# Another order table for a fused linear-attention and gated-MLP kernel on one core

## The chip, the cores and the metric

The kernel runs on one core of a Trainium2 chip. The metric is the device time of one execution in microseconds (us). A core has five engines that take their instructions in order, each from a queue of its own: TensorE (PE, matmuls; its weight loads are listed as PEld), VectorE (DVE), ScalarE (ACT), GpSimd (POOL) and SyncE (SP, which here issues nearly all DMAs). Semaphores order them against each other. Matmul results stand in eight PSUM banks; all other tiles stand in SBUF.

## The reference

There are two parts. The first is a recurrence for 4 batches and 8 heads over 768 positions with head size 48; the second is a gated MLP over all heads joined (width 384).

```
# attention, per batch b and head h
state = alpha[t][:, None] * state + outer(k[t], v[t])      # 48 x 48
y[t]  = q[t] @ state
# MLP, x = y of all heads joined: (4, 768, 384)
h = relu(x @ w_in)                       # 384 -> 1024
u, v = h[..., :512], h[..., 512:]
v_n = (v - mean(v)) / sqrt(var(v) + 1e-6)
v_s = einsum('ts,bsd->btd', w_spatial, v_n) + b_spatial    # mixes positions, 768 x 768
out = (u * v_s) @ w_out                  # 512 -> 384
```

All inputs and the output are float32.

## The kernel before

The sequence is cut into 24 chunks of 128 positions, six for each of the four batches. Inside a chunk the recurrence is written as matmuls: alpha's logarithms are summed by a triangular matmul (`cum`), their exponentials scale q and k (`qt`, `kt`), the scaled q and k are transposed (`tr`, `trk`), multiplied with each other (`sc`), masked (`m`, `ms`) and multiplied with v (`y`); the state that a chunk adds is a matmul of k and v (`upd`), which DVE and POOL carry on (`z`, `S`, `sb`). Chunks 0 to 3 and 6 to 9 are done four at a time with positions interleaved, chunks 4 and 5 as a pair, and all others singly. A batch's chunk outputs (`xe`) then go through the MLP: `v` and `u` products with their ReLU copies (`ve`, `ue`), statistics (`bn`, `rs`, `nm`, `vn`), mixing over positions (`s`, with `se` and the gate product `g`) and the output product (`o`, copied by `oe`, stored by `st`). Weights arrive as float32, are cast to bf16, and the spatial weight is also transposed (`wt`, copied by `we`).

Matmuls use TensorE in several shapes: the full 128x128 array (most MLP products), 64x128 (transposes and `sc`), 128x32 (`y`), 32x32 (`pm`, which rearranges v), 32x128 (`upd` of four chunks), 64x32 and 64x64 (the pair).

The kernel first makes a list of 944 operations. Each has its dependencies, the engines that may run it and a function that emits its instructions. The order of all instructions then comes from one string, `PLAN`. The function `replay` goes through its words from left to right:

```
        op, eng = ops[int(word[1:])], LETTERS[word[0]]
        for x in junk:
            warm(int(cols), int(n), kind)
        for slot, n in zip(op.take, banks):
            held[n] = slot
        op.emit(eng)
```

So `A116` emits operation 116 on ACT, `P410@1,6` emits 410 on PE into banks 1 and 6, and `P62@0:512#0` first emits a dummy float32 matmul of 512 columns into bank 0. The letters D, G and S stand for DVE, POOL and SP. The words of one engine give its queue; the order between engines is left to semaphores. A PE operation that takes a bank waits for the copies that emptied the bank's last content.

The words that the text below speaks of:

| word | operation |
|---|---|
| P62, P66, P75 | running sums of the first four chunks' logarithms |
| P52 | spreads b_spatial over partitions |
| P115, A116 / P128, A129, A135 | v of chunk 0 rearranged and copied / the same of chunks 2 and 3 |
| A102 | copy of transposed q (chunks 0 to 3) |
| A173, A176, A178, A180 | logarithm and exponentials of the pair, chunks 4 and 5 |
| P120, P419 | output of chunk 0, of chunk 10 |
| S12, S16 | loads of w_in, v half and u half |
| S20, S23, S26, S29 | loads of w_spatial in thirds, and of w_out |
| P154, P156, P160 | u products of batch 0, first half of the positions |
| P217, P221 | u products of batch 0, second half |
| S278 | last load of chunks 6 to 9 (v) |
| S494, S560, A564 | alpha loads of chunks 12 and 15, logarithm of chunk 15 |
| P293, A294, G306 | running sum, exponential and scaled key in chunks 6 to 9 |
| G299, G302 | copies of v in chunks 6 to 9 |
| P321, D322 (S.6) | state update of chunks 6 to 9, and its first scaling |
| P410 | transposes of chunks 10 and 11 |

The float32 loads of the weights share two staging buffers, so that a load waits for the casts of the load two before it; the loads of alpha, k, q and v go to a ring of three places.

Of the kernel before, what the change touches and what calls it, by code (L numbers as in the profile page):

```python
# [39 lines left out]


PLAN = """
D2 D0 D4 D1 G9 G11 G5 G6 D3 S56 S57 S59 S58 A60 S12 S169 S170 A61 S275 S171 D8 P62@0:512#0:512#0:512#0 P66@1 P67 P63
P70@2 P71 P74@3 P75 A68 A64 D79 G82 P91@4,5 P52@6 A69 A72 A76 G7 A78 A92 A84 A65 G88 G87 A73 A77 D85 D90 D81 D93 D53
D83 D80 P103@6,4,5,7:512#7:424#7 P94@0,1 D86 D104 D89 D106 G13 P97@6,2:192#2 D98 A95 P100@3,0 D101 A96 P117@3,6:376#1
P115@4,1 A99 G107 G14 A15 A173 D102 D109 P128@0,2 D119 D118 P174@5 A116 A122 A176 P130@6,4 S16 D132 D131 S172 A135
P175@1 A129 P120@3 P54@2 G110 G105 P136@0,4 A121 A178 A55 G111 G108 P133@6 G181 A180 A134 G184 A179 D112 A177 D138
P123@7,3 P141@2 S20 G279 G280 G281 G17 G19 G18 D124 D125 P151@6 P187@7,4 P126@3 S23 S277 S276 D185 A152 A127 G186 G183
G113 G114 D182 P190@5,6 A189 A192 A142 P144@3 D137 P139@4 D188 D191 A140 G22 G21 D153 D143 P199@6,5 P196@2,7 P162@4
A283 A145 P290@0 A163 P154@1 P160@3 A282 A291 A155 D200 D201 D198 D197 D164 P193@4 A161 P156@7 A157 A165 D194 D146  # L50
P158@5 A159 G195 P202@1,2 P203 S26 A204 A147 D166 P293@4 P37@5,7 D38 P34@3,6 G24 S278 S387 S399 G25 S506 S29 D35
P207@1 D148 D208 D36 A39 A292 P205 P284@7 P40@3,5 A206 A285 A167 G10 D42 P210@2 D149 D150 D41 S388 S389 D168 D209 S401
S400 P287@5 P223@6 P219@3 P221@1 A211 A294 A224 A288 D212 A286 A220 A213 D298 D304 A289 A295 D214 D222 D215 A216
P225@6 P233@2 P217@3 P229@7 P237@0 A218 A28 D301 G300 G27 D307 G297 P226 D227 G303 G306 P43@3,5 D45 P230 P234 D231
D235 A296 A44 P46@4,6 P309@5,1 D311 P238 P49@7,3 D50 D51 A48 A47 A310 P312@2,6 P318@1,4 P315@5,7 P249@3 P250 A313 A319
A317 A299 A314 A302 D316 D320 D239 G236 D251 P341@4,1 P335@7,5 P245@0 P246 G305 G308 D336 D342 G232 P321@7,6,3,2 G240
G228 D343 D322 A510 G33 D337 D324 D247 P253@4 P333@7,1 P254 P241@5 P242 G323 A391 A403 A30 A340 A334 A32 G325 P392@0
D255 P348@7,6 D243 D327 D350 A393 P344@4 A394 P338@5 G31 G328 D397 D330 D349 G396 P404@3 A345 A339 A405 A406 P257@1
A395 S495 S390 A258 P260@4 P359@2 S402 G407 G248 G326 G329 S494 S560 P346@0,7 D408 P354@3,5 P410@1,6 A360 D331 A347
A353 A411 D356 D355 P362@2 G252 G398 P351@7 A352 P357@3 D412 S508 S497 S509 P421@6,1 P416@5,0 D361 S496 S507 S562 S550  # L60
S548 S611 S561 S551 S549 A358 A363 D418 D423 P511@7 P369@3 P413@0 P374@2 P380@1 D414 D417 A261 A512 P378@0 D422 A498
D364 A375 A564 P263@5 P499@6 G244 G332 G409 G256 A370 A379 A513 D371 G415 A500 A501 P419@0 P424@3 A425 G517 G505 G503
D381 D382 D516 G515 A420 P266@2 P269@4 A502 A365 A383 A270 D366 D504 P429@0 P426@1 P438@3 P440@6 D384 A368 A430 A427
P436@4 A437 A441 A385 D264 D439 P272@0 D367 D267 D428 D431 D386 P521@1 P372@4 A514 A273 P565@6 P376@2 A377 A432 A552
P442@7 A568 P529@0 D443 D522 P456@3 D433 D434 A435 A566 A567 D373 P452@7 P553@1 P518@2,5 A519 A554 A556 D520 A555 P457
D458 D530 D570 G569 G523 G557 G459 P444@4 P445 P448@5 D446 P453 D454 P468@6 P449 D558 D450 P533@7,4 P524@2,0 P572@1,3
D525 G451 G455 P472@5 P469 P460@2 P473 D526 D534 D535 G531 G447 D474 S623 A559 P575@7 D576 A573 P461 S625 S612 S563
A615 D470 D462 P616@4 P527@5 P536@1 A627 S613 A574 P579@7,3 P588@6,0 G577 A617 A528 D589 A618 A537 P628@5 A629 A571
G475 P538@2 A630 P464@1 S624 S614 S730 S718 S721 S626 S720 G620 D621 D581 D580 S733 S732 P476@6 G631 G578 P541@3
P584@7 A539 A619 A542 P465 S784 S719 A477 D632 P634@5,4 D590 A636 D466 D585 S731 A722 P591@3 S786 S772 S785 S773 S835  # L70
S774 A592 S787 S775 G622 G532 P582@1 A583 D635 D540 P637@7 P482@6 A633 A483 P723@5 G586 G471 D638 G639 A724 P645@3,4
P640@0,2 D543 G463 G587 P479@7 P604@6 P596@1 D646 D642 D641 A734 A726 D647 G729 G467 A605 A741 G727 P593@3 P600@6 A594
P735@0 D606 D595 A738 D480 P648@4 P643@3 A544 D545 D546 D597 A649 P488@2 A644 A788 A601 A489 D547 P653@4 P660@7 P745@6
A654 D746 D655 A736 A607 D608 D610 P491@3 P664@4 A661 A665 A737 P650@6 A492 A776 G739 P598@1 D651 D609 P485@4 D652
A486 A725 D747 P666@7 A667 D740 P602@6 P662@4 P789@3 A656 A603 P676@7 P672@0 P753@6 A599 A790 A791 P777@1 A778 A792
A779 S484 S847 S836 S837 A839 A783 S838 S848 A663 S849 D657 D658 D659 D754 D728 P677 P673 P680@6 P688@5 D674 P681
P668@0 D794 D755 D678 D782 G781 G795 D682 P799@7 P669 G793 D800 P689 G675 D690 D670 P742@6,4 P796@7,3 A851 A780 D797
P696@5 A743 A798 G683 G679 P808@0 P697 P852@7 P840@6 A841 A842 A853 A843 A854 D744 P748@3,4 P757@1,2 D698 G801 G671
D749 D809 D758 P692@5 P693 D694 D750 P684@3 P703@0 P685 P700@5 G846 D759 A701 D686 P706@4 D856 D845 D707 A704 P760@5
A761 P751@0 A752 A802 P803@6,7 D805 G844 G855 P812@3,2 P858@4,5 G810 G687 G699 G691 A859 G695 D813 P762@0 S850 P861@7  # L80
P765@3 D814 D804 P712@2 P815@6 A756 A763 P806@0 A860 D862 D764 D857 A816 A807 A766 P864@5,7 P869@4,1 S702 P715@6 D866
D871 D767 D870 D865 P828@7 A829 D830 P824@1 P820@3 P817@7 A821 A768 A818 A825 G863 P872@4 A873 S705 A716 S481 S259
S268 S487 S265 S493 S490 S271 S708 S262 S478 S274 G811 P867@5 D819 P826@3 P822@1 D868 P877@4 D769 D771 A827 S717 A831
A823 A878 A770 A713 D832 P874@3 D833 D834 P890@5 P888@1 P884@4 D879 D875 D876 A880 D881 D882 P916@6 P709@2 A710 P896@3
P886@7 P900@0 A887 A889 A885 A891 P892@2 D883 P897 D898 G899 P893 P901 P908@5 P909 D894 D902 P904@2 P905 G903 P917
P912@0 P913 P920@3 D906 D895 D918 G919 D907 P929@6 P923@2 P921 S711 A930 S931 A924 S925 S714 D914 D910 D911 P926@6
G915 D922 P932@2 A933 D927 S928 S934 P938@3 D939 S940 P935@6 A936 S937 P941@3 D942 S943
"""


# [1174 lines left out]
```

## Time and profile before

| | |
|---|---|
| runs | 138.22, 138.32, 139.34 us; median 138.32 |
| span of the profiled execution | 137.9 us (no other time is given for it) |
| instructions in the profile | 5298 |
| first matmul that isn't a dummy | 6.37 us after the span's start |
| DMA | 28.66 MB in 76521 packets, mean 208 GB/s |
| loads of one chunk of alpha, k, q or v | 192.0 KB, median 4.2 to 4.4 us from issue to landing |
| granted TensorE clock | 9 tenths or more in every slice |

The times in the profile count from the span's start. A row of the timeline gives start, length, engine, line, operation, output and inputs with their shapes, and how many instructions of one kind were merged in it; in brackets stands the idle time before it and what ended it. Starts are measured; the ends of matmuls are modelled, so that the distance between starts is what a matmul costs in a stream. A row of busy time by stage gives the stretch, its length, each engine's busy time with the number of its instructions, the granted clock, the DMA share and the DMA rate.

### The profile page before, as it was taken

What the parts mean: (1) busy time and instruction counts of PE and PEld (TensorE: products, weight loads), DVE (VectorE), ACT (ScalarE), POOL (GpSimd) and SP (SyncE); (2) the same over time, 40 slices, a digit from 0 to 9 for tenths busy, and PEclk for the clock granted to TensorE, in tenths of its full rate; (3) what the DMA queues carried; (4) which work ended last, traced back from release to release, by engine and by line L of the source; (5) the groups of instructions that cost most, each with busy time, mean ns of one, the idle gap of its engine ahead of it and who ended that gap; (6) DMA issues with size and microseconds to landing.
All of it is one profiled execution on the core that took longest, in us unless ns stands there. A gap on an engine that the chain in (4) does not pass through costs nothing.

```text
span 137.9 us, 5298 instructions
## 1 busy us (share of the span) xinstructions
PE 130.1 (94%) x2108; PEld 79.4 (58%) x2122; DVE 120.2 (87%) x300; ACT 107.7 (78%) x261; POOL 86.6 (63%) x146
## 2 busy tenths in 40 slices
PE   6999998999999999799999999999999999999990
PEld 3365555565566556466657676656576765566560
DVE  6259999989989999899899999997999999974960
ACT  3476998999999799699997989999865796953040
POOL 7355899993499799761079989520799841004550
PEclk9999999999999999999999999999999999999999
DMA  3999999499989788699999898999960597101064
GB/s 88 370 372 381 344 349 361 106 373 382 355 162 281 159 168 165 124 186 188 193 204 201 164 209 156 189 186 216 213 134 5 187 349 270 63 0 57 0 233 172
DMA packets 76521, 28.66 MB, mean 208 GB/s; under 512 B 63056, under 2 KB 74960, under 8 KB 76496
## 3 DMA queue, kind: packets, MB, share of 16 engines
q1 hardware_dynamic: 76464, 28.32, 77.8%
q8 instruction: 16, 0.26, 0.8%
q14 instruction: 9, 0.07, 0.2%
q0 software_dynamic: 32, 0.00, 0.0%
HBM read 23.60 MB, written 4.72 MB: 205 GB/s over the span
## 4 chain that ended last, share of the span: by engine, by line
PE 60%; DMA 19%; POOL 8%; issue 3%; SPq 3%; ACT 3%; DVE 0%; POOLq 0%; ACTq 0%
PE bank L1005 43%; DMA raw_w<-in_moe_w_spatial_dram 6%; DMA kc<-in_k_dram 5%; DMA raw_w<-in_moe_w_out_dram 4%; DMA ac<-in_alpha_dram 4%; PE bank L960 3%; SPq L883 3%; PE bank L944 2%; PE bank L988 2%; PE bank L416 2%; POOL w_row L180 2%; POOL kt L189 2%; PE bank L932 1%; PE bank L898 1%; POOL state L189 1%
## 5 line engine op out<-in xcount | busy, mean ns | idle before, releaser
L1005 PE MATMUL bank<-w_spT,vn 128*128 128x384 bf16 x192 | 35.6, 327 | 0.0
L189 POOL TENSOR_TENSOR gT<-vs,uT 128x384 bf16<-128x384 f32 x28 | 25.7, 933 | 14.1 <-DVE vs L1152 14.1
L189 POOL TENSOR_TENSOR kt<-kc,binv 128x384 bf16<-128x384 f32 x22 | 20.2, 928 | 22.3 <-ACT binv L908 15.2
L1005 PEld LDWEIGHTS <-vn 128*128 128x128 bf16 x192 | 17.5, 98 | 11.2 <-issue 0.3
L1005 PE MATMUL bank<-w_in,xT 128*128 128x512 bf16 x58 | 17.4, 380 | 1.6 <-ACT xT L178 0.7
L1005 PE MATMUL bank<-xT,w_in 128*128 128x384 bf16 x96 | 18.7, 326 | 0.0
L1005 PE MATMUL bank<-w_out_sb,gT 128*128 128x384 bf16 (+1 forms) x100 | 18.4, 320 | 0.0
L1152 DVE TENSOR_TENSOR vs<-bank,bsp_bc 128x384 f32<-128x384 f32 x31 | 16.3, 549 | 2.4 <-PE bank L1005 2.3
L949 DVE TENSOR_TENSOR ptm<-bank,mask 128x512 bf16<-128x512 f32 x28 | 17.9, 682 | 0.5 <-PE bank L944 0.3
L178 ACT COPY kqT<-bank 128x512 bf16<-128x512 bf16 (+1 forms) x20 | 15.0, 793 | 3.1 <-PE bank L988 1.9
L1067 DVE BATCH_NORM_STATS2 stats<-v_sb 128x6 f32<-128x512 bf16 x24 | 16.4, 683 | 0.6 <-ACT v_sb L184 0.5
L184 ACT ACTIVATE v_sb<-bank 128x512 bf16<-128x512 f32 x20 | 11.7, 597 | 2.0 <-PE bank L1005 1.7
L184 ACT ACTIVATE uT<-bank 128x384 bf16<-128x384 f32 x27 | 12.4, 494 | 0.7 <-PE bank L1005 0.6
L1005 PEld LDWEIGHTS <-w_in 128*128 128x128 bf16 x96 | 9.0, 97 | 6.7 <-DVE ptm L949 0.3
L189 DVE TENSOR_TENSOR qt<-qc,bank 128x384 bf16<-128x384 f32 x24 | 12.6, 545 | 0.2 <-DMA qc<-in_q_dram 0.2
L1005 PEld LDWEIGHTS <-gT 128*128 128x128 bf16 x100 | 9.2, 98 | 5.8
L178 ACT CAST xT<-bank 128x384 bf16<-128x384 f32 x23 | 10.4, 482 | 1.1 <-PE bank L416 0.8
L843 DVE TENSOR_TENSOR ptm<-bank,mask 128x512 bf16<-128x512 f32 x16 | 10.3, 683 | 0.2 <-PE bank L836 0.2
L242 PE MATMUL bank<-junk 128*128 128x512 f32 (+3 forms) x14 | 8.8, 763 | 1.0 <-DVE junk L1231 1.0
L1005 PEld LDWEIGHTS <-xT 128*128 128x128 bf16 x72 | 6.2, 97 | 6.2 <-ACT xT L178 1.2
L178 ACT COPY raw_w<-bank 128x384 f32<-128x384 f32 x8 | 3.8, 479 | 7.3 <-PE bank L1005 7.2
L393 DVE TENSOR_TENSOR zs<-bank,state 128x384 f32<-128x384 f32 x16 | 8.8, 548 | 0.5 <-PE bank L932 0.4
(162 smaller groups left out, 264.3 us busy)
## 6 DMA issues: line engine op xcount, KB each, us to landing
ac<-in_alpha_dram SPq DMA_DIRECT2D x14, 192.0 KB, 4.4
kc<-in_k_dram SPq DMA_DIRECT2D x14, 192.0 KB, 4.4
qc<-in_q_dram SPq DMA_DIRECT2D x14, 192.0 KB, 4.4
vc<-in_v_dram SPq DMA_DIRECT2D x14, 192.0 KB, 4.2
raw_w<-in_moe_w_spatial_dram SPq DMA_DIRECT2D x3, 768.0 KB, 7.8
out_dram<-raw_w SPq DMA_DIRECT2D x11, 192.0 KB, 2.1
out_dram<-o_sb SPq DMA_DIRECT2D x9, 192.0 KB, 2.0
ac<-in_alpha_dram SPq DMA_DIRECT2D x2, 768.0 KB, 6.7
```

The costliest lines, as they stand in the source:

```text
L178: nc.scalar.copy(out=out, in_=in_)
L184: nc.scalar.activation(out=out, in_=in_, func=AF.Relu)
L189: ENG[eng].tensor_tensor(out=out, in0=in0, in1=in1, op=ALU.mult)
L242: nc.tensor.matmul(out=banks[n][:, 0:cols].rearrange("p (a b) -> p a b", a=4), lhsT=junk, rhs=junk[:, None, 0:cols // 4].to_broadcast([128 ...
L393: lambda _: nc.vector.tensor_tensor(out=zs[i % 3], in0=tp(), in1=state[(i - 1) % 3], op=ALU.add),
L843: nc.vector.tensor_tensor(out=ptm[n2][:, ci, s], in0=banks[sl.bank].rearrange("p (hp t) -> p hp t", hp=HP), in1=mask[:, 3][:, None, :].to_ ...
L883: nc.sync.dma_start(out=t[x].rearrange("p hp s d -> p (hp s) d"), in_=src[b, :, c * C:c * C + C, :].rearrange("h s d -> s h d"))
L949: nc.vector.tensor_tensor(out=ptm[n2][:, ci, s], in0=banks[sl_p[s].bank].rearrange("p (hp t) -> p hp t", hp=HP), in1=mask[:, 2][:, None, : ...
L960: nc.tensor.matmul(out=place(to, 3 * hp + (0, 1, 1, 2)[x]), lhsT=heads(vb, hp, x), rhs=ptm[n2][:, ci, x // 2, hp, :], start=(turn == 0), s ...
L1005: nc.tensor.matmul(out=ps, lhsT=lhsT, rhs=rhs, start=first and n == 0, stop=last and n == len(pairs) - 1)
L1067: nc.vector.bn_stats(out=stats[tt % 2], in_=v_sb[n2][:, tt, :])
L1152: nc.vector.tensor_tensor(out=vs[d], in0=banks[sl.bank][:, 0:TH], in1=bsp_bc[:, th, :], op=ALU.add)
```

## The change

Only `PLAN` is new. Its 944 words name the same operations. No operation, tile or dependency is added or removed. What differs:

- the order on all five engines, and with it the bank numbers;
- the engine of some elementwise operations: DVE has 225 words in place of 235, ACT 240 in place of 234, POOL 115 in place of 111; PE has 265 and SP 99 as before;
- the dummy matmuls: before they were 512, 512, 512 | 512, 424 | 192 | 376 columns, and they are 512, 512, 512, 120 | 328 | 512 | 144 | 456 | 288 | 248 | 512, 96 (a bar parts places in the order);
- successive PE words of different tile shape: 78 places in place of 85, dummies counted as the full shape.

```diff
 PLAN = """
-D2 D0 D4 D1 G9 G11 G5 G6 D3 S56 S57 S59 S58 A60 S12 S169 S170 A61 S275 S171 D8 P62@0:512#0:512#0:512#0 P66@1 P67 P63
-P70@2 P71 P74@3 P75 A68 A64 D79 G82 P91@4,5 P52@6 A69 A72 A76 G7 A78 A92 A84 A65 G88 G87 A73 A77 D85 D90 D81 D93 D53
-D83 D80 P103@6,4,5,7:512#7:424#7 P94@0,1 D86 D104 D89 D106 G13 P97@6,2:192#2 D98 A95 P100@3,0 D101 A96 P117@3,6:376#1
-P115@4,1 A99 G107 G14 A15 A173 D102 D109 P128@0,2 D119 D118 P174@5 A116 A122 A176 P130@6,4 S16 D132 D131 S172 A135
-P175@1 A129 P120@3 P54@2 G110 G105 P136@0,4 A121 A178 A55 G111 G108 P133@6 G181 A180 A134 G184 A179 D112 A177 D138
...
-P158@5 A159 G195 P202@1,2 P203 S26 A204 A147 D166 P293@4 P37@5,7 D38 P34@3,6 G24 S278 S387 S399 G25 S506 S29 D35
...
-A317 A299 A314 A302 D316 D320 D239 G236 D251 P341@4,1 P335@7,5 P245@0 P246 G305 G308 D336 D342 G232 P321@7,6,3,2 G240
...
-A395 S495 S390 A258 P260@4 P359@2 S402 G407 G248 G326 G329 S494 S560 P346@0,7 D408 P354@3,5 P410@1,6 A360 D331 A347
...
-D364 A375 A564 P263@5 P499@6 G244 G332 G409 G256 A370 A379 A513 D371 G415 A500 A501 P419@0 P424@3 A425 G517 G505 G503
...
-G915 D922 P932@2 A933 D927 S928 S934 P938@3 D939 S940 P935@6 A936 S937 P941@3 D942 S943
...
+G11 D2 D1 G7 S56 D4 D0 S57 G5 G8 A60 P66@0:512#0:512#0:512#0:120#0 G6 P62@1 A61 P63 A64 A65 P70@2 P71 A72 P74@3 P67
+A68 P75 A76 D79 D3 P52@4 A53 G85 G88 S59 A81 G90 D82 P91@5,6:328#5 A92 S58 D84 D87 D93 P103@5,6,4,7:512#7 D80 A69 D83
+G9 A73 D86 S16 G18 A78 D104 A77 D89 P97@1,0:144#1 A99 A98 G105 A19 P100@3,0:456#2 P94@1,5 D106 G107 D101 S169 A173
+G108 P128@6,2 A135 A102 A129 G17 S12 D96 D95 P117@1,5:288#3 P174@3:248#3 P175@2 S170 A176 D109 G110 G14 D118 D119
+P130@0,1 D131 D132 D112 A180 A178 P115@5,4 A116 P120@5:512#6:96#6 S171 P123@1,0 D124 A121 A177 A179 P133@7 A134 A122
...
+G181 P187@7,0 D189 D138 P144@5 P160@2 D153 G113 P154@1 P156@3 A188 A145 D146 A161 S275 G279 G280 A282 A157 P199@5,7
...
+P219@5 A220 P233@6 P217@2 P293@0 P229@1 D212 D298 A213 S26 S278 S494 S29 D214 D216 D215 S399 P221@3 S400 A292 D304
...
+D337 D251 D247 D336 D342 P253@6 P254 A498 G299 G302 P321@1,3,2,4 D322 D324 P333@7,0 A334 S401 A340 D255 P241@5 P242
...
+G396 P410@0,6 P263@7 A261 D356 G398 G329 D347 P351@3 A353 P357@4 D411 A412 A510 P416@6,0 P421@5,1 S560 A352 P372@3
+A358 D361 D417 D422 G252 D418 A264 P413@4 G331 D414 A500 D364 G244 S508 A501 A564 P511@6 P380@7 P369@5 A502 D423 A381
...
+A942 S943
 """
```

More of the change, by code (lines that the diff above doesn't have):

```diff
@@ L63 @@
[L63 to L86, printed above, removed]
-G915 D922 P932@2 A933 D927 S928 S934 P938@3 D939 S940 P935@6 A936 S937 P941@3 D942 S943
+G11 D2 D1 G7 S56 D4 D0 S57 G5 G8 A60 P66@0:512#0:512#0:512#0:120#0 G6 P62@1 A61 P63 A64 A65 P70@2 P71 A72 P74@3 P67
```

52 lines of the change are left out of this document (39 added, 13 removed).

## The prediction

> **What bounds the kernel now.** I read the page's busy shares first, then busy time by stage, then the chain that ended last, and last the timeline of single engines. The shares of the whole span:
>
> ```profile
> span 137.9 us, 5298 instructions
> PE 130.1 (94%) x2108; PEld 79.4 (58%) x2122; DVE 120.2 (87%) x300; ACT 107.7 (78%) x261; POOL 86.6 (63%) x146
> ```
>
> These average over stages with different limits, so the next view is busy time by stage (length, PE, PEld, DVE, ACT, POOL, granted clock, DMA share, GB/s):
>
> ```profile
> 0.00:20.00 20.00, 18.50 (x281) 10.04 (x283) 14.41 (x58) 13.65 (x31) 13.26 (x33) 1.00 0.97 315
> 20.00:30.00 10.00, 9.25 (x254) 5.61 (x257) 9.52 (x22) 9.48 (x22) 9.78 (x15) 1.00 0.84 279
> 30.00:40.00 10.00, 9.84 (x135) 5.45 (x130) 9.76 (x28) 9.59 (x25) 5.88 (x11) 1.00 0.99 320
> 40.00:49.00 9.00, 8.95 (x232) 5.67 (x225) 8.52 (x19) 7.94 (x20) 8.04 (x12) 1.00 0.86 201
> 49.00:60.00 11.00, 9.81 (x219) 6.30 (x220) 10.11 (x21) 9.48 (x24) 9.18 (x15) 1.00 0.82 160
> 60.00:80.00 20.00, 19.89 (x258) 12.71 (x259) 18.91 (x44) 18.17 (x47) 12.26 (x16) 1.00 0.97 192
> 80.00:100.00 20.00, 19.84 (x286) 12.46 (x286) 18.93 (x48) 18.68 (x51) 11.14 (x17) 1.00 0.97 195
> 100.00:120.00 20.00, 19.73 (x387) 12.70 (x389) 19.48 (x43) 15.22 (x36) 11.84 (x15) 1.00 0.53 173
> ```
>
> From 60 us on TensorE (PE) lacks 0.11, 0.16 and 0.27 us of each 20: it sets the end, and only less work on it, or an earlier arrival at 60 us, is worth anything. From 20 to 49 us it loses 0.75, 0.16 and 0.05 us, with VectorE (DVE) and ScalarE (ACT) nearly as full. From 49 to 60 us it loses 1.19 us, and nearly all of that is one wait. The 18.50 us of the first stage flatter it, since they hold dummy matmuls. The chain names the one wait (start, length, what; then the ACT and PE timelines of that place):
>
> ```profile
> 51.62 5.70 DMA ac<-in_alpha_dram
> 57.41 0.52 ACT L888 ACTIVATE la<-ac 128x384 bf16<-128x384 f32 x1 [1.09 <-DMA ac<-in_alpha_dram]
> 58.85 0.35 PE L960 MATMUL bank<-ptm,vb 128*32 128x128 bf16 x12 [1.03 <-ACT uT L184]
> ```
>
> The logarithm of chunk 15 (A564) stands in ACT's queue 1.09 us for a load that left at 51.62. Behind it wait the copies that free PSUM banks, and P419 (chunk 10's output) starts 1.03 us late.
>
> **Changes of shape.** I counted them in both tables word by word, dummies as the full shape: 85 before, 78 after. By PE work done, both have 18 in the first 9.3 us; the next 27 us have 33 before and 28 after, the rest 34 and 32. The price stands in PE's timeline:
>
> ```profile
> 16.48 0.32 PE L466 MATMUL bank<-la,le_pair 128*128 128x384 bf16 x1 [0.20 <-ACT la L448]
> 16.64 0.32 PE L466 MATMUL bank<-la,lt_pair 128*128 128x384 bf16 x1
> 18.25 0.33 PE L1032 MATMUL bank<-b_sp_sb,ones_row 1*128 1x384 bf16 x1
> 18.51 0.40 PE L836 MATMUL bank<-kqT 48*128 48x128 bf16 x8
> 72.61 0.40 PE L988 MATMUL bank<-ident,kt 64*128 64x64 bf16 x16
> 72.85 0.40 PE L988 MATMUL bank<-ident,qt 64*128 64x64 bf16 x16
> 73.18 0.34 PE L1005 MATMUL bank<-w_spT,vn 128*128 128x384 bf16 x1
> ```
>
> A 384-column matmul is followed by its like after 0.16 us and by another shape after 0.26; sixteen transposes by sixteen more after 0.24 us and by the full shape after 0.33. So a change costs about 0.095 us both ways, and seven fewer give **-0.67 us**. The two ends are -0.2 (only the two in the PE-bound rest count, the others lie beside DVE's work) and -0.67.
>
> The Trainium skill, page "TensorEngine Tiling (Array Packing)", section "Key Properties", says that changing the tiling mode drains TensorE. "TensorE: Matmul & The Clock Gate", section "Single matmul latency", has a lone warm matmul cost (398+N)/2.4 ns; an estimate by that page takes 166 ns a change, and seven would be 1.2 us instead. The quoted starts give 95 ns, so I stay with those.
>
> **The first 25 us.** ACT takes its queue in order. Before, chunk 0's value copy (A116) follows the logarithm A173 directly; after, A135, A102, A129, A176, A180 and A178 come between. Their intervals:
>
> ```profile
> 13.61 1.56 ACT L178 COPY kqT<-bank 128x512 bf16<-128x512 bf16 x3 [1.07 <-PE bank L771]
> 15.04 0.64 ACT L178 CAST w_in<-raw_w 128x512 bf16<-128x512 f32 x1
> 16.31 0.87 ACT L178 CAST vb<-bank 128x384 bf16<-128x384 f32 x2
> 17.05 0.51 ACT L495 ACTIVATE binv<-bank 128x384 bf16<-128x384 f32 x1
> 17.43 0.88 ACT L178 CAST vb<-bank 128x384 bf16<-128x384 f32 x2
> 19.53 0.37 ACT L504 ACTIVATE bc<-bank 64x8 f32<-64x8 f32 x2
> 17.91 0.41 PE L854 MATMUL bank<-ptm,vb 128*32 128x128 bf16 x16
> 14.73 0.90 PE L242 MATMUL bank<-junk 128*128 128x376 f32 x2
> ```
>
> Two value copies at 0.37, a key-query copy at 0.48, two exponentials at 0.38 and a small pair at 0.37 make 2.35 us. A116 then runs from about 16.31 + 2.35 = 18.7 to 19.2, and P120 (chunk 0's output, at 17.91 before) starts 1.3 us later, with PE work ahead of it only 0.2 us more. So PE is 1.1 us behind. The dummies say alike: those between P75 and P120 grow from 1504 to 2584 columns, and 376 columns took 0.90 us with the pipeline's end, about 1.67 ns a column without it: 1.8 us more at most. The first matmul too stands behind 120 more dummy columns.
>
> Of this I take 0.4 us back by 30 us: P160, P154 and P156 (u products) now stand right behind chunk 1's v product, where PE lost 0.75 us for want of ready work. Sum of the stage **+0.7**, from -0.4 (no loss, but the gain) to +1.8.
>
> **The wait at 57 us.** Between the last four-chunk load (S278) and chunk 15's decay (S560) stand 12 loads in the old queue of SP, 10 in the new, of 0.197 MB each beside w_out. The rate there and the hole before it (lengths as above):
>
> ```profile
> 44.80:62.00 17.20, 15.94 (x307) 9.83 (x309) 16.05 (x34) 14.68 (x39) 13.96 (x22) 1.00 0.82 161
> 24.10:27.60 3.50, 3.27 (x55) 2.03 (x54) 3.39 (x7) 3.44 (x8) 3.44 (x7) 1.00 0.47 112
> 18.34 7.18 SPq L1047 DMA_DIRECT2D raw_w<-in_moe_w_spatial_dram  x2
> 23.40 1.72 POOL L180 CAST w_in<-raw_w 128x512 bf16<-128x512 f32 x3
> ```
>
> Two loads at 161 GB/s are 2.4 us, more than the 1.09 waited. The hole at 24 us comes from S23, held on SP until POOL had cast w_in's u half. The new table loads that half first, so S23 should pass; S20 then depends on the v half's casts, with some 2 us of transfers still queued. ACT's own work ahead of A564 grows only 0.4 us. So the wait goes, **-1.07 us**; what is late next is P410 and its neighbours, which follow DVE (in the rival below). Ends: 0 to -1.2, all that PE loses there.
>
> **Moved engines.** DVE gets ten instructions fewer, ACT six more, POOL four more. By the stage rows all three stay below PE from 60 us on, so I take 0; the ends are -0.5 (what PE loses from 60 to 120 us) and +0.3 (ACT, at 18.68 of 20, late with a bank a few times).
>
> **The end.** The last copy goes from DVE to ACT:
>
> ```profile
> 134.02 0.48 ACT L178 COPY raw_w<-bank 128x384 f32<-128x384 f32 x1 [0.50 <-PE bank L1005]
> 134.35 0.36 DVE L180 COPY raw_w<-bank 128x192 f32<-128x192 f32 x1 [0.62 <-PE bank L1005]
> ```
>
> ACT is busy until 134.50 with its own copy; its intervals are 0.1 shorter than its lengths, so +0.05 us, between 0 and +0.2. The order of the last matmuls and stores stays.
>
> Sum: -0.67 + 0.7 - 1.07 + 0.05 = -1.0 us on the profiled execution's span, 137.9 to 136.9. The median of the runs shown, 138.32, lies 0.4 above that span, and no other time of the execution is given; the same difference gives **137.3 us**.
>
> **Rivals.** *The start costs nothing (faster still).* If the old table's late eviction order was as bad as the new one's, the stage gives -0.4, and relieved DVE saves the 0.5 late: -0.67 - 0.4 - 1.07 - 0.5 = -2.6, 135.7 us. For it: DVE has 9.76 of 10 us from 30 to 40 and loses work. Against it: the ACT queue before P120.
>
> *A late update (slower than before).* P321, the update of chunks 6 to 9, needs every scaled key and value copy of that group.
>
> ```profile
> 29.33 0.34 PE L711 MATMUL bank<-la,le_quad 128*128 128x384 bf16 x1
> 35.44 0.91 POOL L189 TENSOR_TENSOR kt<-kc,binv 128x384 bf16<-128x384 f32 x1 [3.12 <-ACT uT L184]
> 41.47 0.95 POOL L180 CAST o_sb<-vc 128x384 bf16<-128x384 f32 x2
> 43.72 0.86 PE L794 MATMUL bank<-o_sb,kt 32*128 32x96 bf16 x64
> 50.20 0.55 DVE L189 TENSOR_TENSOR qt<-qc,bank 128x384 bf16<-128x384 f32 x1
> 51.24 0.40 PE L988 MATMUL bank<-ident,kt 64*128 64x64 bf16 x16
> ```
>
> The new table moves P293 (at 29.33) behind 5.2 us more of PE work, to about 35.2; its exponential A294 follows two u copies, the first of which needs P221, 0.9 us of PE work behind P293, and ends near 38. POOL then has key G306, three gates, a cast and two value copies until G302: 4 x 0.9 + 0.5 + 0.95 = 5.0 us. P321 has 0.6 us more PE work ahead of it than before and the start's 0.7, so its turn comes near 43.72 + 1.3 = 45.0, and PE waits as soon as A294 ends after 40.0. DVE's S.6 waits for P321 in order, with 6 us of DVE work from there to P410, which followed DVE's 50.20 copy closely before: the delay passes on whole. Two us late gives -1.0 + 2 = +1.0, 139.3 us. For it: ACT is full there (9.59 of 10). Against it: POOL's 3.12 us idle can be filled.
>
> *Fewer changes don't count.* They lie beside DVE's work (-0.2), and the late load is replaced by another wait: -0.2 + 0.7 - 0.5 + 0.05 = 0, 138.3 us.
>
> **How the numbers follow.** Forecast 0.45, faster still 0.25, late update 0.18, changes that don't count 0.12. The measurement tells a difference from none at about 1%, here below 136.94 or above 139.70. The forecast's own spread, 136.4 to 138.2, gives 0.1 to faster; with the first rival that is 0.35. Slower is the late update beyond its middle price and a start at its +1.8: 0.13. The rest, 0.52, is no difference. The range reaches to both outer rivals: 135.6 to 139.5.
>
> **What would show it.** Right: PE starts P120 near 19.2; no ACT idle over 0.3 us before A564, and PE from 49 to 60 us over 10.5 busy; starts 95 ns wider only at the 78 changes; P321 near 45. Wrong: P120 at 18 or earlier (start), an ACT or POOL queue waiting for a load between 40 and 60 us, P321 after 46, or PE below 19.6 in a 20 us stage after 60.

## The result: 1.0% slower

| | before | after |
|---|---|---|
| times | 138.27 us median of 4 (138.12 to 139.34) | 140.13 us median of 4 (139.91 to 140.43) |
| ratio, 95% interval | | 1.0104 [1.0073, 1.0135] |
| second measurement, 11 and 6 runs | 138.62 us | 140.46 us, 1.0119 [1.0095, 1.0143] |

A few executions of some kernels are over 1.5% longer than the fastest of the same kernel; the ratios leave them out, the medians do not. The forecast, 137.3 us with a range up to 139.5, was wrong. The page of the changed kernel begins with span, then busy time (share, instructions) of each engine:

```profile
span 138.7 us, 5306 instructions
PE 132.4 (95%) x2119; PEld 80.6 (58%) x2132; DVE 117.3 (85%) x285; ACT 111.0 (80%) x267; POOL 90.1 (65%) x155
```

Beside the 137.9 us of before this looks like 0.8 us lost, and yet the times differ by 1.9. All executions of after have spans 1.7 to 1.8 us below their times (138.7 at 140.43, 138.1 at 139.91), so a span of 137.9 belongs to a time of about 139.7, not to the median of 138.3. The kernel before was therefore profiled again (first experiment). Its second page, of an execution of 138.11 us:

```profile
span 136.3 us, 5312 instructions
PE 130.9 (96%) x2122; PEld 79.3 (58%) x2122; DVE 119.9 (88%) x300; ACT 107.6 (79%) x261; POOL 86.5 (63%) x146
```

Against this one after loses 2.3 us of span (138.65 against 136.34, unrounded). Busy time by stage (length, PE, PEld, DVE, ACT, POOL, clock, DMA share, GB/s), first after:

```profile
0.00:20.00 20.00, 18.81 (x229) 10.28 (x229) 12.64 (x49) 13.21 (x28) 14.03 (x40) 1.00 0.94 303
20.00:30.00 10.00, 9.53 (x223) 5.61 (x226) 9.12 (x21) 9.27 (x22) 9.16 (x13) 1.00 1.07 372
30.00:40.00 10.00, 9.74 (x172) 5.60 (x168) 9.41 (x26) 9.77 (x26) 7.33 (x12) 1.00 1.07 337
49.00:60.00 11.00, 10.89 (x220) 6.94 (x211) 10.55 (x22) 10.36 (x28) 10.17 (x15) 1.00 0.94 186
100.00:120.00 20.00, 19.67 (x360) 12.52 (x362) 19.41 (x42) 16.53 (x35) 13.05 (x17) 1.00 0.41 120
```

and the same stages in the second profile of before:

```profile
0.00:20.00 20.00, 18.50 (x282) 10.04 (x283) 14.49 (x58) 13.76 (x31) 13.37 (x33) 1.00 0.98 318
20.00:30.00 10.00, 9.74 (x259) 5.67 (x258) 9.50 (x23) 9.52 (x23) 9.78 (x15) 1.00 0.87 278
30.00:40.00 10.00, 10.00 (x138) 5.51 (x140) 9.75 (x29) 9.62 (x25) 6.15 (x11) 1.00 1.04 326
49.00:60.00 11.00, 11.00 (x228) 6.80 (x226) 10.77 (x22) 10.64 (x29) 10.26 (x15) 1.00 0.87 171
100.00:120.00 20.00, 20.00 (x337) 12.54 (x332) 19.42 (x43) 15.61 (x35) 10.30 (x13) 1.00 0.45 157
```

Two things are to be seen. From 30 us on an ordinary execution of before has PE full, from 49 to 60 us too: the wait of 1.03 us is not there. And the first stage of after is fuller on PE with 53 fewer matmuls recorded, since more of them are long dummies. DVE does 1.85 us less in it.

Such rows are too coarse for a ledger, so I used **lateness**: the start of a PE operation minus the PE work ahead of it in its own table (distances between starts of like matmuls, 0.095 us for each change of shape, dummies not counted). It stays level while PE streams and steps up at a wait or a dummy. The work is 120.41 us with before's 85 changes and 119.73 with after's 78. Lateness added, in us:

| profile | 9 to 25 us | 25 to 40 | 40 to end |
|---|---|---|---|
| before, second profile | 4.64 | 0.01 | 1.20 |
| after | 6.74 | 0.26 | 1.62 |
| after, second profile | 6.37 | 0.32 | 1.62 |

After's start costs 1.7 to 2.1 us more, 25 to 40 us 0.3, the rest 0.4, and 0.67 is saved. The sum is +1.8 to +2.1; the remaining 0.2 to 0.4 of the spans' difference is the first real matmul (6.32 in before, 6.51 and 6.68 in after). It scatters from 6.10 to 6.75 us over the profiles of all runs, with a mean of 6.42 in the eleven that have 120 dummy columns more ahead of it and of 6.31 in the nine that have not, so at most some 0.1 us of it is the table's. The chain of waits shows where dummies stood on the path in after (start, length, what):

```profile
15.85 0.71 PE bank L243 x2
16.56 0.33 PE bank L837 x8
16.89 0.62 PE bank L243 x2
17.50 0.65 PE bank L467 x4
18.15 0.18 PE bank L472 x8
18.33 0.33 PE bank L837 x8
18.66 0.28 PE bank L815 x8
18.95 1.25 PE bank L243 x4
20.20 0.34 PE bank L855 x16
```

Line 243 is the dummy, 855 is P120. It began at 20.12; in the second profile of before (line 854) at 17.80. PE's and ACT's timelines of after, and PE's of before, at that place; the `vb` cast is A116:

```profile
18.88 1.32 PE L243 MATMUL bank<-junk 128*128 128x512 f32 x4
20.12 0.41 PE L855 MATMUL bank<-ptm,vb 128*32 128x128 bf16 x16
19.13 0.47 ACT L179 CAST vb<-bank 128x384 bf16<-128x384 f32 x1
17.80 0.41 PE L854 MATMUL bank<-ptm,vb 128*32 128x128 bf16 x16
```

### The profile page after: what moved, and what is told of

Its sections match the earlier page's. It is cut to its first block, busy times and chain, and to the rows that moved or that the text cites. A ratio compares the mean times of both kernels' runs of the same rounds, so it can differ in the third digit from the quotient of the medians.

```text
span 138.7 us, 5306 instructions
## 1 busy us (share of the span) xinstructions
PE 132.4 (95%) x2119; PEld 80.6 (58%) x2132; DVE 117.3 (85%) x285; ACT 111.0 (80%) x267; POOL 90.1 (65%) x155
## 4 chain that ended last, share of the span: by engine, by line
PE 84%; ACT 6%; DVE 4%; issue 2%; ACTq 0%; DVEq 0%
PE bank L1006 52%; PE bank L243 7%; PE bank L961 3%; PE bank L989 3%; PE bank L945 3%; PE bank L417 2%; ACT binv L741 2%; PE bank L899 2%; PE bank L837 2%; PE bank L855 2%; PE bank L933 2%; PE bank L772 1%; PE bank L795 1%; DVE o_sb L181 1%; DVE vn L1097 1%
## 5 line engine op out<-in xcount | busy, mean ns | idle before, releaser
L1006 PE MATMUL bank<-w_spT,vn 128*128 128x384 bf16 x192 | 35.1, 326 | 0.2 <-DVE vn L1097 0.2
L179 ACT COPY kqT<-bank 128x1024 bf16<-128x1024 bf16 (+1 forms) x23 | 17.7, 820 | 2.5 <-PE bank L989 1.6
L1006 PE MATMUL bank<-w_out_sb,gT 128*128 128x384 bf16 (+1 forms) x100 | 18.1, 320 | 0.0
L1006 PE MATMUL bank<-w_in,xT 128*128 128x512 bf16 x59 | 16.8, 379 | 0.9 <-ACT kqT L179 0.2
L185 ACT ACTIVATE v_sb<-bank 128x512 bf16<-128x512 f32 x23 | 13.9, 610 | 0.5 <-PE bank L1006 0.4
L243 PE MATMUL bank<-junk 128*128 128x512 f32 (+7 forms) x24 | 11.9, 613 | 1.1 <-DVE junk L1232 1.1
L179 ACT COPY raw_w<-bank 128x384 f32<-128x384 f32 (+1 forms) x11 | 5.1, 474 | 7.9 <-PE bank L1006 7.9
L1097 DVE TENSOR_SCALAR vn<-v_sb,mvs,rstd 128x512 bf16<-128x512 bf16 x20 | 9.1, 491 | 0.0
```

What stands on the lines that cost most here:

```text
L179: nc.scalar.copy(out=out, in_=in_)
L185: nc.scalar.activation(out=out, in_=in_, func=AF.Relu)
L243: nc.tensor.matmul(out=banks[n][:, 0:cols].rearrange("p (a b) -> p a b", a=4), lhsT=junk, rhs=junk[:, None, 0:cols // 4].to_broadcast([128 ...
L1006: nc.tensor.matmul(out=ps, lhsT=lhsT, rhs=rhs, start=first and n == 0, stop=last and n == len(pairs) - 1)
L1097: nc.vector.tensor_scalar(out=vn[n2][:, x, :], in0=v_sb[n2][:, x, :], scalar1=mvs[n2][:, x, 0:1], scalar2=rstd[n2][:, x:x + 1], op0=ALU.su ...
```

## Experiments

Each is told as a change of words of the table. Times are medians; the kernel before ran beside each (138.3 to 138.7).

**1. The kernel before, unchanged, profiled again.**

> The kernel before, unchanged, profiled a second time. Three executions of the kernel after have spans 1.7 to 1.8 us below their times (138.7 at 140.43, 138.1 at 139.91, 138.5 at 140.26). By that the profile of before with its 137.9 us belongs to an execution of 139.6, that is to the one of 139.34 and not to those of 138.22 and 138.32, and its wait of 1.09 us before the logarithm of chunk 15 is an accident of that execution. Theory A (accident): a new profile at a time near 138.2 has a span near 136.5 and no wait over 0.3 us at 57 us; my third step of -1.07 us then had nothing to take. Rival B (the wait is a property of the table): span 137.9 again, the wait of about 1 us again, and the time outside the span is 0.4 here and 1.7 in the kernel after for a reason of its own.

138.65 us, ten runs from 138.09 to 139.47 with spans from 136.3 to 137.7, always 1.7 to 1.8 below the time. The chain of waits around chunk 10:

```profile
54.87 2.27 PE bank L1005 x13
57.14 0.16 PE bank L898
57.30 0.08 PE bank L901 x4
57.38 0.34 PE bank L960 x16
```

and the logarithms in ACT's timeline there:

```profile
54.75 0.55 ACT L888 ACTIVATE la<-ac 128x384 bf16<-128x384 f32 x1
55.78 0.51 ACT L888 ACTIVATE la<-ac 128x384 bf16<-128x384 f32 x1
```

P419 (line 960) follows PE's own work, and the logarithms have no idle time in front. Theory A holds: the first profile showed an execution of about 139.7 us, and its wait of 1.09 us belongs to that execution and not to an ordinary one. Nor is there idle time in front of these logarithms in the profiles of experiments 7, 11 and 12, which keep this part's order. All of these are of executions near the fastest of their kernel; how many of the longer ones have the wait is not known. The table has several levels of time: of its 106 executions on record 21 took 138.1 us, the most frequent value, and 29 took 139.0 or more.

**2. All dummies behind the first real matmul taken out of after.**

```diff
-P91@5,6:328#5 ... P103@5,6,4,7:512#7 ... P97@1,0:144#1 ... P100@3,0:456#2 ... P117@1,5:288#3 P174@3:248#3 ... P120@5:512#6:96#6
+P91@5,6 ... P103@5,6,4,7 ... P97@1,0 ... P100@3,0 ... P117@1,5 P174@3 ... P120@5
```

> The kernel after without its eight groups of dummy matmuls behind the first real matmul (328, 512, 144, 456, 288, 248, 512 and 96 columns, 16 matmuls); the four groups ahead of the first real matmul stay. Theory A (the dummies stand on the path: they are longer than the holes they fill): P120 starts 1.0 to 1.6 us earlier, near 18.8, and the time falls by 0.7 to 1.5 us, to about 138.6 to 139.4. Rival B (they only fill holes that ACT and DVE make): P120 stays within 0.3 us of 20.1 and the time within 0.4 us of 140.1. Rival C (they keep the clock up): the granted clock in the first 30 us drops below 1.0, matmuls there take up to twice as long, and the time rises by 1 us or more.

142.81 us, 1.031 [1.0277, 1.0342]. Rival C holds. Busy time of its stages (the granted clock stands third from the end):

```profile
8.60:12.00 3.40, 1.88 (x38) 1.26 (x36) 2.79 (x7) 3.17 (x9) 2.75 (x4) 1.00 1.09 383
12.00:15.40 3.40, 2.64 (x98) 2.33 (x99) 3.02 (x7) 1.95 (x7) 2.33 (x7) 0.50 1.09 378
22.20:25.60 3.40, 3.40 (x23) 0.81 (x15) 2.68 (x6) 2.13 (x5) 2.83 (x4) 0.50 1.08 383
25.60:29.00 3.40, 3.39 (x79) 2.14 (x79) 2.36 (x5) 2.89 (x6) 2.76 (x6) 0.99 1.05 382
```

PE was busy 1.88 of 3.40 us, the clock went to half, and it came back only behind 3.4 us of full PE. So this start needs dummies, and the question is how long each must be. The Trainium skill, page "TensorE: Matmul & The Clock Gate", section "What's actually happening", has the clock halved after an idle window of about 3.4 us and restored after a busy one. The return agrees; the fall came after 3.4 us in which PE was half busy.

**3. Shorter dummies where the hole was shorter.**

```diff
-P174@3:248#3 ... P120@5:512#6:96#6
+P174@3 ... P120@5:192#6
```

> The kernel after without the dummy of 248 columns ahead of P174, and with 192 columns instead of 512 and 96 ahead of P120; all else as it is. Theory A (these dummies are longer than the holes: P174's logarithm was there 0.9 us before P174 started, and chunk 0's value copy ended 0.5 us before P120 started): P174 at 16.85, P120 at 19.0 to 19.3, granted clock 1.0, time down by 0.7 to 1.1 us to 139.0 to 139.4. Rival B (other work is late at once): P120 0.8 earlier, but P144 within 0.3 us of 25.1 and the time within 0.3 us of 140.1. Rival C (the clock needs them): granted clock below 0.95 somewhere before 30 us and a time over 141.

139.97 us, 1.0096 [1.006, 1.0132], clock 1.00. P120 came 12.77 us behind the first real matmul instead of 13.61. Of these 0.84 us 0.2 to 0.5 reached the time (139.97 against after's two medians, 140.13 and 140.46), and the intervals overlap, so that no gain is shown. In the profiled execution they were lost again at once:

```profile
24.43 0.19 PE L536 MATMUL bank<-ident,kt 64*128 64x64 bf16 x1 [0.90 <-issue]
24.55 0.82 PE L1006 MATMUL bank<-w_in,xT 128*128 128x512 bf16 x3
```

The last key transpose of chunk 2 (P187) stands 0.90 us for something that the profile does not name, and P144 comes 18.39 behind the first real matmul, between the 18.58 and 18.27 of after's two profiles. The time lies between theories A and B.

**4. Chunk 0's and 1's values in their old turn.** This also takes out the dummies that experiment 3 left ahead of P120, and undoes the very step that my forecast blamed.

```diff
-P128@6,2 A135 A102 A129 ... P174@3:248#3 ... P115@5,4 A116 P120@5:512#6:96#6 ... A134 A122
+P115@6,2 A116 A102 A122 ... P174@3 ... P128@5,4 A129 P120@6 ... A134 A135
```

> The kernel after with the value products and copies of chunks 0 and 1 (P115, A116, A122) in the places of those of chunks 2 and 3 (P128, A129, A135) and the other way round, as their turn comes in the kernel before; the dummies ahead of P174 and P120 are left out, as no hole should be there. Theory A (the place of A116 in ACT's queue delays P120): P120 at 17.9 to 18.5 instead of 20.1, time 138.3 to 139.2. Rival B (P120's order is not what the later stages wait for): P120 near 18.3, but P144 within 0.5 us of 25.1, and a time above 139.5.

139.89 us, 1.0088 [1.0055, 1.0121]. P120 came 1.2 us earlier (12.42 behind the first real matmul), but the lateness at 25 us fell by 0.3 to 0.7 only. The time is that of rival B. PE now waits one operation later:

```profile
18.52 0.41 PE L855 MATMUL bank<-ptm,vb 128*32 128x128 bf16 x16
19.75 0.40 PE L837 MATMUL bank<-kqT 48*128 48x128 bf16 x8 [0.82 <-DVE ptm L844]
```

**5. The two tables joined in four ways.** Banks behind the joint were dealt out anew by the time they come free.

```diff
+ (the first 140 words of before, to P144) (all other words in after's order)
+ (the first 130 words of after, to P144) (all other words in before's order)
+ (the first 195 words of before, to P207) (all other words in after's order)
+ (as the first, with P160 P154 P156 moved behind P162)
```

The first:

> The table of before up to and with P144 (its first 140 words, dummies and banks with them), then all other words in the order and on the engines of the table after, with PSUM banks dealt out anew by the time they come free. Theory A (the loss sits in the start: P144 at 22.9 instead of 25.1): most of the 2.2 us comes back, time 138.0 to 138.8. Rival B (the rest of the new order loses: from 60 us on PE stalls more, 1.0 us against 0.6): time 139.3 or more. If both hold in equal parts, about 139.

The second, its mirror:

> The mirror: the table after up to and with P144, then all other words in the order of before, banks dealt out anew. Theory A (the start costs): 139.8 to 140.5, about the kernel after. Rival B (the rest costs): about 138.3 to 138.8, since a start 2.2 us late would be caught up in the holes at 24, 27 and 57 us.

The third:

> The table of before up to and with P207 (30 us), then all other words in the order and on the engines of the table after, banks dealt out anew. The first mixture, cut at P144, lost 1.9 us at 24 to 26 us because its u products P160 and P154 stood ahead of the cast of w_in's u half, which the old start makes late; cut at P207 they lie in the old part. Theory A (the whole loss is in the new table's first 30 us): P207 at 29.9 instead of 33.1, time 137.5 to 138.1, at or below before. Rival B (what the new order does after 30 us loses another us by itself, 0.4 at P234 and 0.6 in small waits): 138.6 to 139.2.

The fourth:

> The first mixture (table of before through P144, then the new order), with the three u products P160, P154 and P156 moved from behind P144 to behind P162, so that they do not wait for the cast of w_in's u half. 78 changes of shape. Theory A (the new order behind 25 us is sound, and the mixture's loss was that wait of 1.9 us): P207 at 30.0 to 31.0, time 137.6 to 138.3, at or below before. Rival B (the new order behind 25 us needs the loads and the engine queues of its own start): new waits between 25 and 42 us, time 139 or more, as when the tables were joined at 30 us (141.2).

139.68, 139.97, 141.19 and 143.28 us. The mirror runs without a wait at its joint: after's start before the rest of before adds a lateness of 6.21 by 25 us, nearly as in after, and the ratio is 1.0116 [1.009, 1.0142]. So after's start is enough for a loss of this size. Each mixture with the old start made a wait of its own; in the first one PE's u products met casts that the old start makes late:

```profile
24.07 0.34 PE L1005 MATMUL bank<-xT,w_in 128*128 128x384 bf16 x1 [0.52 <-POOL w_in L180]
25.18 1.51 PE L1005 MATMUL bank<-xT,w_in 128*128 128x384 bf16 x7 [0.78 <-POOL w_in L180]
```

In the third PE stood 0.80 us for ACT's copy of a chunk output and 0.68 for a cast of w_spatial on POOL. In the fourth it stood 1.62 us for ACT's copy of `kqT`, and in four of the six executions the clock fell to half for a while (the two others took 142.34). So these three tell little of the new order's rest; none of these joints had it without a new wait.

**6. Changes of shape added to before.** Twelve swaps of neighbours in PE's order, such as

```diff
-P335@7,5 P245@0
+P245@0 P335@7,5
```

> The kernel before with twelve pairs of neighbouring PE operations swapped between 42 and 116 us, such that each swap adds two changes of tile shape: 109 changes instead of 85, the same work. Theory A (a change costs 0.095 us and PE sets the end): 24 x 0.095 = 2.3 us more, time 140.3 to 140.9. Rival B (a change is hidden by work beside it): within 0.5 us of 138.3. Rival C (0.166 us each): 4.0 us more, 142.3.

145.05 us, 1.0451 [1.0411, 1.049]: none of the three theories holds. The last output product began 6.5 us later than in before; 24 changes at 0.095 are 2.3 of it, and the other 4.2, by subtraction, are waits, since the operation moved forward comes before its operands or its bank:

```profile
111.11 0.41 PE L960 MATMUL bank<-ptm,vb 128*32 128x128 bf16 x16 [0.57 <-ACT o_sb L178]
```

The price of a change alone is not isolated by this. What it shows is that moving an operation forward by one place in PE's order cost more here, 0.35 us on average, than the two changes that came with it would at 0.095 each. The price can be read from the traces without an experiment: in nine profiles, behind 28 us, the distance from a matmul group to the next is 0.09 to 0.10 us longer where the shape changes than where it does not, in 12 of the 14 kinds of change that are frequent enough to compare (0.07 in the other two; compared at the 30th percentile, where few waits come in).

**7. After's grouping by shape put into before.** P94 (chunk 0's query transposes) behind its likes P97 and P100, P130 behind P175.

```diff
-P94@0,1 D86 ... D98 A95 P100@3,0 D101 A96 ... P130@6,4 S16 D132 D131 S172 A135 P175@1
+D86 ... D98 P100@3,0 P94@4,1 A95 D101 A96 ... P175@1 P130@6,4 S16 D132 D131 S172 A135
```

> The kernel before with two groupings of the new table put into it and nothing else: P94 moved behind P97 and P100 (with its banks and its first copy A95), and P130 moved behind P175. 83 changes of shape instead of 85. Theory A (this grouping is what costs the start): P117 0.6 to 1.0 us later than 15.45, P144 0.8 to 1.4 later than 22.6, time 139.0 to 139.8. Rival B (the two saved changes are all it does): 0.2 us less, 138.1. Rival C (PE's later holes absorb it): P117 late, P207 on time, 138.3.

141.56 us, 1.0195 [1.0153, 1.0237]; the two executions with an undisturbed clock took 140.76 and 140.88. Against the 138.1 of before's fastest executions, two moves that save two changes cost 2.7 us. ACT's and PE's timelines:

```profile
15.37 1.56 ACT L178 COPY kqT<-bank 128x512 bf16<-128x512 bf16 x3 [2.70 <-PE bank L771]
16.50 0.90 PE L242 MATMUL bank<-junk 128*128 128x376 f32 x2 [1.14 <-ACT kqT L178]
17.33 0.40 PE L836 MATMUL bank<-kqT 48*128 48x128 bf16 x8
```

ACT's next copy is that of P94, so ACT stands idle for 2.70 us with copies behind it that could run, and P117 starts at 17.33 instead of 15.45. After's own table puts other copies there, and pays less.

**8. The grouping undone in after** (with experiment 4). A first try gave P97 a bank that was read until 15.05; the second has other banks, and its 192 dummy columns stand ahead of P97 in place of P100.

```diff
-P103@5,6,4,7:512#7 D80 A69 D83 G9 ... P97@1,0:144#1 A99 A98 ... P100@3,0:456#2 P94@1,5 ... P174@3 P175@2 ... P130@0,1
+P103@5,6,4,7:512#7 D80 A69 D83 P94@1,0 G9 ... A95 P97@2,5:192#2 A96 ... P100@3,1 D98 A99 ... P174@3 P130@1,0 A122 P175@4
```

The first try:

> The kernel after with its start undone where it groups PE operations of one shape: P94 (chunk 0's query transposes) goes back to right behind P103 instead of behind P97 and P100, and P130 (chunk 2's scores) to between P174 and P175 instead of behind both; the copies that follow P94 and P97 go back to the engines of before, chunk 0's and 1's values keep the turn they have in the run with the exchanged value copies, and the dummies between P103 and P120 shrink to 192 and 288 columns. Theory A (grouping by shape puts operations that feed VectorE and ScalarE behind others, and these engines then idle): P117 at 15.5 to 15.8 instead of 16.5, P120 near 17.9, P162 1.0 to 1.6 us earlier than in the run with the exchanged copies, time 138.3 to 139.2. Rival B (from 20 us on ACT's queue sets the pace whatever the start): P117 early, but P207 within 0.4 us of that run's and a time of 139.6 or more.

The second:

> The order of the run with P94 and P130 put back, with other PSUM banks: in that run P97's transposes were given the bank that chunk 1's second q product still read until 15.05, and the copies behind it went late. Here P97 takes the bank of chunk 0's first state column. Theory A (the place of P94 and P130 costs the start): from the first real matmul to P117 9.1 to 9.3 us as in the kernel before (after: 9.7), to P144 16.4 to 17.0, time 138.5 to 139.3. Rival B (POOL's queue binds next: w_in's casts stand ahead of chunk 2's key products): P117 9.2 us behind the first matmul, but P187 and P144 not earlier than in the run with the exchanged value copies (17.2 and 17.6 us), time 139.6 or more.

140.53 and 140.18 us (1.0153 [1.0114, 1.0192] and 1.0131 [1.0084, 1.0178]). In the second P120 started at 18.41, but two of its six executions, the profiled one among them, lost the clock:

```profile
20.00:22.00 2.00, 0.81 (x30) 0.40 (x18) 1.70 (x4) 1.39 (x4) 2.00 (x4) 0.96 1.10 364
22.00:24.00 2.00, 2.00 (x5) 0.38 (x4) 1.04 (x3) 0.97 (x2) 2.00 (x3) 0.50 1.06 323
```

These took 141.59 and 141.77, the four others 139.94 to 140.28. Executions with such a fall are also among those of experiments 4, 5, 7 and 9.

**9. The halves of w_in and POOL's queue, alone and with 8; after itself beside them.**

```diff
-S16 G18 ... A19 ... G17 S12 ... G110 G14 ... A178 ... A135 D182 D125 D185 G13 G15 ... G111 G184 G181
+S12 G14 ... A15 ... G13 S16 ... G110 G181 ... A178 G184 ... A135 G111 D182 D125 D185 G18 G17 G19
```

After itself:

> The kernel after, unchanged, as the base for the three others on this chip: 139.9 to 140.5 us, ratio 1.010 to 1.014. Against the profile of after its first PE matmul should lie between 6.1 and 7.2 us (the landing of the first loads differs from execution to execution), and P144 18.3 to 18.7 us behind it.

The exchange, with experiment 4:

> The run with the exchanged value copies, and in it the two halves of w_in exchanged in loads and casts (the v half first, as before), with chunk 2's key products G181 and G184 ahead of the u half's casts on POOL. P94 and P130 stay where the new table has them. Theory A (POOL's queue costs the start): G184 ends near 20 us instead of 21.3 to 22.2, P187 runs without a wait, P144 16.6 to 17.0 us behind the first real matmul instead of 17.6, time 138.6 to 139.3. Rival B (the place of P94 and P130 binds): P144 still 17.5 us behind the first matmul, time 139.6 or more. If DMA binds: P160 waits for the u half's casts by over 0.5 us, and the time is above 140.

The exchange, with the second try of experiment 8:

> Both: P94 and P130 put back, and the halves of w_in and the key products exchanged. If the two causes add, P144 lies 16.2 to 16.5 us behind the first real matmul, as in the kernel before (16.3), and the time is 137.9 to 138.5: the seven saved changes are then worth no more than the small waits that the new order has behind 35 us. If a third cause is left, over 139.

140.46, 140.80 and 140.30 us. Three of the six executions of the exchange with experiment 4 lost the clock; the others took 139.94 to 140.14. Neither cause alone nor both gave the start back. With both, P120 began at 18.07, and the next wait took it:

```profile
21.11 0.82 PE L1006 MATMUL bank<-w_in,xT 128*128 128x512 bf16 x2 [1.08 <-ACT vb L179]
```

P141's operands were there at 19.52; it waits for the copy A135 (20.53 to 21.06) that empties its bank.

**10. That bank, and all behind it, dealt out anew.**

```diff
-P141@5 P54@1 ... P136@4,3 P126@5 ... P190@1,2 ... P187@7,0 ... P144@5
+P141@2 P54@6 ... P136@0,5 P126@1 ... P190@3,4 ... P187@6,2 ... P144@7
```

> The run with both causes undone, and PSUM banks dealt out anew from P141 on by the time they come free: there P141 waited 1.2 us for the bank of chunk 3's second value copy (A135, ended 21.05, P141 started 21.11). Theory A (each cure was eaten by the next wait, the last of them this bank): P141 near 20.0, P144 16.7 to 17.1 us behind the first real matmul instead of 18.1, time 138.7 to 139.3. Rival B (ACT's queue, which the chain of waits follows from 24 to 38 us, sets the pace): P144 early, P234 as far behind the first real matmul as before the change of banks, time 139.8 or more.

139.36 us, 1.0042 [1.0011, 1.0072], 1.1 under after's second median, but not for the reason of theory A alone. The start's lateness fell to 5.71 and P144 came at 23.23, 1.4 earlier than in the run before it. P234 did not move (38.60 against 38.66), as rival B has it, though the chain names DVE's normalisation and not ACT:

```profile
37.47 1.09 DVE vn L1097 x2
38.55 0.04 issue
38.60 0.50 PE bank L1006 x2
```

What the time gained came behind 40 us, where the new banks cut the lateness from 1.6 to 0.97.

**11. A known delay in before.** The dummies that after has ahead of P120, here in bank 3:

```diff
-P120@3
+P120@3:512#3:96#3
```

> The kernel before with the two dummies that the new table has ahead of P120 (512 and 96 columns), nothing else: PE reaches P120 1.0 us later. Theory A (the table has no slack to take a late start back, since PE is full from 30 us to the end): P144 and the last matmul 0.9 to 1.1 us later, time 139.2 to 139.7. Rival B (holes at 22 to 25 us take back some 0.4, as my forecast had it): 0.5 to 0.7 us, 138.9 to 139.2. Rival C (all absorbed): within 0.2 us of before.

PE's timeline at that place:

```profile
17.68 1.30 PE L242 MATMUL bank<-junk 128*128 128x512 f32 x4
18.91 0.41 PE L854 MATMUL bank<-ptm,vb 128*32 128x128 bf16 x16
```

P120 began at 18.91 (1.11 later), P144 1.13 later, the last output product 1.14 later; most executions took 139.20 to 139.36, where before's fastest took 138.06 to 138.09; the ratio is 1.0079 [1.0041, 1.0118]. Theory A holds: nothing is taken back.

**12. Before with new banks behind P144.** 178 of its words get another bank; order, engines and dummies stay.

> The kernel before with its order, engines and dummies unchanged, and PSUM banks dealt out anew behind P144: each operation takes the free bank that came free first in the second profile of before. In three runs in which the banks behind the joint or behind P144 were dealt so (the mixture joined at P144, its mirror, and the run with new banks from P141) PE's small waits from 40 us to the end sum to 0.8 to 1.0 us, against 1.6 in after with its own banks and 1.2 in before, and the time between a bank's coming free and its next matmul has a median of 0.84 us instead of 0.40. Theory A (part of PE's small waits is for banks): 0.3 to 0.5 us less than before, 137.6 to 137.9, and fewer executions above 139, since a late load finds more slack. Rival B (operands set those waits): within 0.2 us of before.

138.24 us against 138.69, 0.9977 [0.9955, 0.9999], lowest 137.89 against 138.08. That is 0.2 to 0.45 us below before, and the interval only just excludes no gain; the size is about that of theory A, though the time is not in its 137.6 to 137.9. Lateness from 40 us to the end fell from 1.20 to 0.87. The last columns of the ledger for the other runs:

| profile | 9 to 25 us | 25 to 40 | 40 to end |
|---|---|---|---|
| before, new banks | 4.65 | 0.01 | 0.87 |
| before with the delay | 5.66 | 0.17 | 1.21 |
| before with the grouping | 6.97 | 0.37 | 1.21 |
| after, dummies cut (3) | 6.48 | 0.46 | 1.63 |
| after, values in old turn (4) | 6.07 | 0.49 | 1.61 |
| after, both causes undone (9) | 6.49 | 0.55 | 1.63 |
| the same, new banks (10) | 5.71 | 1.28 | 0.97 |
| old start, new rest, new banks | 6.31 | 0.73 | 0.95 |
| new start, old rest, new banks | 6.21 | 0.52 | 0.81 |

The last column depends on the banks: 1.6 with after's, 1.2 with before's, 0.8 to 1.0 in the four tables of this list whose banks were dealt by the time they come free, in either order. The third and fourth mixtures of experiment 5, which are not in this list, lose 1.5 us there although their banks were dealt likewise, 0.5 to 0.6 of it before 50 us; whether their joints do that is not settled.

## Why the prediction was wrong, step by step

In spans of the profiled executions (138.11 us before, 140.43 and 140.31 after) the forecast had -1.0 us and the measurement is +2.2 to +2.3. The steps that failed are the wait at 57 us (1.07 taken that was not there), the first 25 us (1.0 to 1.4 too little), and what the sum put at nothing behind 25 us (0.7 lost); the first real matmul adds 0.2 to 0.4, mostly scatter.

**The base.** I set the span of 137.9 us beside the median of 138.32 and read an offset of 0.4. The offset is 1.7 to 1.9 in every execution that shows both. The profile was of an execution well above the median, and I used its waits as the table's.

**The wait at 57 us (-1.07).** This step failed, for that reason. After has no such wait either (PE 10.89 of 11 us, as forecast), but in an ordinary execution of before there was nothing to take, so the step is worth 0.

**The first 25 us (+0.7).** This step is right in sign and partly in mechanism, and failed in size: it cost 1.7 to 2.1. P120 was to start at 19.2 and started at 20.12. A116 did come late, and ended near 19.6 where I had 19.2; the dummies ahead of P120 (1.32 us for a hole of some 0.7) added the rest. I had counted these columns and kept them as a bound only. The 0.4 taken back by 30 us failed outright: experiment 11 shows that none of a known 1.11 comes back. And P120 was not the one late operation: experiments 4, 8, 9 and 10 moved it to 18.5, 18.4, 18.1 and 18.1, and each time another wait stood behind it (DVE's masks, the clock, a bank). With the last bank freed the start gave back 0.7 to 1.0, and the stretch from 25 to 40 us took it again (1.28 instead of 0.3). What holds that stretch is not settled, and neither is which of the start's waits would have to go first: the mirror of experiment 5 shows that the start as a whole is enough for the loss, and no single cause in it gave the loss back.

**Changes of shape (-0.67).** The price is right (0.09 to 0.10 us, experiment 6), and the ledger stays level between waits with it; that seven changes fewer shorten the time by 0.67 is not shown by an experiment of its own, since every edit that moved a change moved an operand too. What I missed is how changes are saved: like operations are put together, and one that feeds ACT or DVE goes behind its likes. Experiment 7 prices that in the old table at 2.7 us for two changes saved.

**Moved engines (0).** The 0.4 us lost behind 40 us is not theirs: it goes with the banks in both orders, and after's order and engines with new banks lose 0.95 to 0.97, where before's lose 0.81 to 0.87, so that some 0.1 is left for them. My steps behind 60 us look at the order of the words, and none at the numbers behind the @.

**The end (+0.05).** Nothing came of it: from the start of the last output product to the end of the span it is 4.04 and 4.05 us in both profiles of before, and the same in both of after.

**The rivals.** "A late update" named the right side and the wrong place: P321 was late (46.58, past the 46 that was to prove me wrong), with a lateness already 2.6 us above before's at 40 us, for other reasons. "The start costs nothing" is refuted by the ledger, and "fewer changes don't count" is not borne out: the changes keep their price.

## What to carry to other kernels

Before a gain is booked from a wait in a profile, see that the profiled execution is an ordinary one: its span plus the usual offset has to give the median. In this table, which fills PE to the end, a start that is 1 us late stays 1 us late. The first operations that feed the vector engines were worth 1.7 to 2.1 us here and the saved changes 0.67, so group like matmuls only where what is put off has slack. Look at bank numbers apart from the order: dealing PSUM banks by the time they come free took about 0.3 us from a tuned table without moving one instruction, little above the noise.

## What the runs showed that I had not expected

- In four profiles the clock falls to half, for 3.41 us or for four times that, and each time the 3.41 us before the fall had PE busy for 1.48 to 2.25 us. Busy time alone does not decide it: of the stretches of 3.41 us that follow one another from the clock's first rise, others with 1.91, 2.19, 2.21 and 2.27 us busy were followed by no fall (the first from 30.01 us on in the fourth mixture of experiment 5). A borderline start gives two levels of time over executions, 1.5 us apart, at the same table.
- In the second profile of before half of the PE operations behind 30 us took a bank within some 0.4 us of its coming free, while their operands had been ready for about 1.7 us in the median. In this kernel banks are scarcer than operands, and still new banks were worth only about 0.3 us.
- Single executions of one table differ by up to 1.4 us (138.09 to 139.47) at a clock of 0.99 to 1.00. The first profile of before, of about 139.7 us, shows one possible cause, a late load met by a queue in order; others were not looked for.
